# A new priority table and new TensorE costs for the list schedule of an attention and feed-forward kernel

## The chip, the core and the metric

The kernel runs on one core of a Trainium2 chip. The metric is the device time of one execution in microseconds. Three runs of the kernel before gave 746.95, 749.21 and 749.82 us, a median of 749.21. TensorE (PE in the profile) multiplies and writes to PSUM, VectorE (DVE), ScalarE (ACT) and GpSimd (POOL) do the rest, and SyncE (SP) issues most transfers.

## The reference, cut to what matters

For each of 8 batches and 8 heads (576 tokens, width 64, 32 memory slots):

```
a     = softmax(phi) over the tokens          # 576 x 32
k_m   = a^T k ;  v_m = a^T v                  # 32 x 64 each: the memory
attn  = softmax(q k_m^T / 8) over the slots   # 576 x 32
x     = attn v_m                              # 4608 x 512 over all heads and batches
out   = relu(x w_in)^2 w_out                  # w_in 512 x 2048, w_out 2048 x 512
```

The two weight matrices arrive as 64-bit floats and are decoded on the chip.

## The kernel before, in words

The program is written as a list of 3692 operations with their reads and writes. An operation has for each engine that may run it a cost in nanoseconds (`ways`), and a function that issues its instructions. Nothing is issued when an operation is declared: `Plan.order` schedules the whole list in Python while the kernel is built, and the instructions are then issued in the order found. So the costs never reach the chip. They decide three things: the order of the instructions on each engine, the engine where an operation has a choice, and how many filler matmuls go in.

`forward` is a greedy list scheduler. It takes the engine that can start something first, and on it, among the operations whose inputs and buffers are ready, the one with the lowest rank. Where it finds TensorE idle, the gap is noted, and `emit` puts a filler matmul of 512 columns (`fill`, tile `idle`) in for every 260 or 400 ns of it.

In the kernel before, the ranks come from several places. A first rank is worked out backwards from due times; six rounds of `forward` and `backward` improve it; then the table `PLACES` (1600 numbers, start times of some earlier schedule) replaces the ranks of the first 1600 operations, and six more rounds follow. The best schedule of all is issued.

The work itself: for each batch `memory` (twice, four heads each) makes k_m and v_m: a maximum by DVE, two transposes by TensorE (L570, L573), an exponential, the sums (L594; L591 for batches 0 and 1), 20 matmuls on tiles of 32 columns (L582), and two transposes (L616 or L625, and L629). Batches 0 and 1 then run `attention_turned` (transposes of q L682 and L691, scores L710 and L699, transposes of the result L725 and L733), batches 2 to 7 `scores` (L793, tiles of 64 columns, four operations a batch) and `attention`. `vw` multiplies v_m into a slice of w_in (L754, tiles of 64 rows and 32 columns). `mm1` then is six matmuls of 256 or 320 columns into one of two PSUM banks `h` (L864), followed by relu and square on ACT or DVE; `mm2` multiplies by w_out into four banks `acc` (L899, L900, L902), and `mm2_left` does the last 64 tokens of two batches (L925). `decode` turns a piece of the weights from 64 to 32 bits with several DVE and ACT operations (L500 to L516). For batches 2 to 7 the PSUM results of `memory`, `scores` and one half of `vw` share a single bank, tag `pa.0`.

Of the kernel before, what the change touches and what calls it, by code (L numbers as in the profile page):

```python
# [20 lines left out]
P = 128  # L21
# [6 lines left out]
FIRST = 1100  # L28
# [9 lines left out]
AHEAD = 2000  # L38
BEGIN = {"PE": 1000.0, "DVE": 1100.0, "ACT": 800.0, "POOL": 2100.0, "SP": 800.0}
# [94 lines left out]


class Op:
    __slots__ = ("ways", "fn", "deps", "users", "late", "cap", "left", "start", "gap", "lead", "port", "size", "seq", "slack", "code")


class Plan:  # L140
# [930 lines left out]
```

## Time and profile before

| | us |
|---|---|
| median of three runs | 749.21 |
| the profiled execution, its own time | 749.23 |
| its span, first to last instruction | 747.3 |
| TensorE matmul busy | 733.1 (98%) |
| VectorE busy | 513.4 (69%) |
| ScalarE busy | 311.1 (42%) |

The span is 1.9 us shorter than the execution's time. Matmuls are pipelined: one lasts 0.40 us in the trace and the next starts 0.23 us after it, so busy time says that TensorE had something in flight, and the spacing of starts says how fast it went.

### The profile page before, as it was taken

To read this page: it belongs to the slowest core of one execution; us is meant where nothing else is said; L and a number is where in the kernel's file an instruction comes from. 1 tells how busy PE (TensorE), PEld (TensorE's weight loads), DVE (VectorE), ACT (ScalarE), POOL (GpSimd) and SP (SyncE) were. 2 spreads that over 40 slices of the span, in tenths; PEclk is the share of its full clock that TensorE was granted. 3 is DMA by queue.
4 is the path that set the end of the run, shared out by engine and by line. 5 is a ranking of instruction groups with operands and counts; after the bars stand their busy time and mean duration, and the time that the engine had idled before them with its cause. 6 is when DMAs were issued, how large, how long until landed. Compare 5 with 4: busy or idle time off the path is not lost.

```text
span 747.3 us, 13089 instructions
## 1 busy us (share of the span) xinstructions
PE 733.1 (98%) x5004; PEld 586.9 (79%) x5009; DVE 513.4 (69%) x1200; ACT 311.1 (42%) x723; POOL 56.6 (8%) x132
## 2 busy tenths in 40 slices
PE   7899999999999999999999999999999999999997
PEld 4568888888878887788868888687877888788886
DVE  4889998944677677846767666955677576775551
ACT  3467997845422323523423323423242342443320
POOL 2000000010010000400014000120003200040000
PEclk9999999999999999999999999999999999999999
DMA  9994545260640036400363015410344102220002
GB/s 235 239 255 115 167 145 144 89 172 16 171 148 17 1 81 152 104 1 1 106 154 90 1 52 135 105 46 1 80 115 120 36 1 65 61 58 0 1 1 70
DMA packets 59997, 66.38 MB, mean 89 GB/s; under 512 B 18400, under 2 KB 48096, under 8 KB 59936
## 3 DMA queue, kind: packets, MB, share of 16 engines
q1 hardware_dynamic: 55904, 56.77, 30.0%
q0 software_dynamic: 3552, 8.13, 4.2%
q8 instruction: 39, 0.64, 0.4%
q10 hardware_dynamic: 480, 0.66, 0.4%
q14 instruction: 22, 0.18, 0.1%
HBM read 56.10 MB, written 9.44 MB: 88 GB/s over the span
## 4 chain that ended last, share of the span: by engine, by line
PE 92%; DMA 1%; ACT 0%; DVE 0%; issue 0%; ACTq 0%
PE h L864 28%; PE acc L899 16%; PE acc L902 16%; PE acc L900 16%; PE accl L925 6%; PE vwpv L754 4%; PE psc L793 2%; PE pkv L582 2%; DMA raw<-in_moe_w_out_dram 1%; PE psc L710 1%; PE pq L682 0%; PE vwpa L754 0%; PE pvt L625 0%; PE pvt L629 0%; PE pkv L594 0%; PE pmx L570 0%
## 5 line engine op out<-in xcount | busy, mean ns | idle before, releaser
L864 PE MATMUL h<-ath,vw 128*128 128x320 f32 (+1 forms) x1024 | 208.9, 298 | 0.9 <-ACT r L868 0.9
L899 PE MATMUL acc<-wo,gh 128*128 128x512 f32 x512 | 205.4, 401 | 0.0
L900 PE MATMUL acc<-wo,gh 128*128 128x512 f32 x512 | 201.0, 393 | 0.0
L864 PEld LDWEIGHTS h<-ath,vw 128*128 128x128 f32 x1024 | 168.6, 189 | 29.2 <-issue 7.2
L902 PE MATMUL acc<-wo,glo 128*128 128x512 f32 x512 | 159.9, 399 | 0.0
L870 ACT ACTIVATE gh<-r 128x512 fp32r<-128x512 f32 x128 | 81.0, 633 | 151.3 <-DVE r L869 116.2
L899 PEld LDWEIGHTS acc<-wo,gh 128*128 128x128 f32 x512 | 96.3, 188 | 28.2 <-issue 8.1
L902 PEld LDWEIGHTS acc<-wo,glo 128*128 128x128 f32 x512 | 91.9, 189 | 24.7 <-issue 7.5
L900 PEld LDWEIGHTS acc<-wo,gh 128*128 128x128 f32 x512 | 96.5, 188 | 17.2
L864 PE MATMUL h<-atl,vw 128*128 128x320 f32 (+1 forms) x512 | 109.5, 295 | 0.0
L869 DVE TENSOR_SCALAR r<-h 128x256 f32<-128x256 f32 (+1 forms) x104 | 47.4, 456 | 75.2 <-PE h L864 74.4
L868 ACT ACTIVATE r<-h 128x256 f32<-128x256 f32 (+1 forms) x152 | 61.2, 410 | 89.2 <-PE h L864 80.3
L874 DVE TENSOR_TENSOR glo<-r,gh 128x512 fp32r<-128x512 f32 x128 | 88.0, 687 | 13.7 <-ACT r L872 9.7
L864 PEld LDWEIGHTS h<-atl,vw 128*128 128x128 f32 x512 | 82.3, 189 | 0.0
L873 DVE TENSOR_TENSOR r<-r 128x576 f32<-128x576 f32 x69 | 52.2, 757 | 28.9 <-ACT gl L871 26.4
L961 POOL DMA_DIRECT2D out_dram<-o x84 | 41.4, 501 | 195.8 <-ACT o L428 187.4
L925 PE MATMUL accl<-wo,gl 128*128 128x512 f32 x192 | 48.0, 396 | 0.0
L925 PEld LDWEIGHTS accl<-wo,gl 128*128 128x128 f32 x192 | 35.5, 188 | 11.5 <-issue 4.0
L872 ACT ACTIVATE r<-r 128x576 f32<-128x576 f32 x59 | 40.5, 686 | 1.2
L754 PE MATMUL vwpv<-wi,VT 64*32 64x512 f32 (+1 forms) x264 | 34.9, 588 | 0.7 <-DVE wi L510 0.7
L754 PE MATMUL vwpa<-wi,VT 64*32 64x512 f32 (+1 forms) x264 | 34.9, 588 | 0.0
L871 ACT ACTIVATE gl<-r 128x64 fp32r<-128x64 f32 x128 | 31.5, 246 | 4.8 <-DVE r L869 4.5
(133 smaller groups left out, 700.9 us busy)
## 6 DMA issues: line engine op xcount, KB each, us to landing
raw<-in_moe_w_out_dram SPq DMA_DIRECT2D x16, 512.0 KB, 3.6
KV<-in_v_dram SPq DMA_DIRECT2D x16, 512.0 KB, 5.6
KV<-in_k_dram SPq DMA_DIRECT2D x16, 512.0 KB, 4.3
raw<-in_moe_w_in_dram SPq DMA_DIRECT2D x32, 256.0 KB, 4.3
q<-in_q_dram SPq DMA_DIRECT2D x24, 304.0 KB, 4.4
q<-in_q_dram SPq DMA_DIRECT2D x24, 240.0 KB, 3.9
out_dram<-o POOLq DMA_DIRECT2D x80, 64.0 KB, 2.0
phi<-in_phi_dram SPq DMA_DIRECT2D x16, 256.0 KB, 5.7
```

Source lines behind the costliest of these rows:

```text
L754: nc.tensor.matmul(ps_[hh]()[32 * s:32 * s + 32, 0:n], V()[pr, s, :], W()[pr, s, c0:c0 + n], start=True, stop=True, tile_position=(64 * hh ...
L864: nc.tensor.matmul(p()[:, 0:n], V()[:, l, hh, c0:c0 + P], x()[:, hh, cs], start=(i == 0), stop=(i == 5))
L868: op({"ACT": act(n), **({} if b < 2 else {"DVE": tt(n)})}, lambda e, cs=cs, n=n, p=p: nc.scalar.activation(r()[:, cs], p()[:, 0:n], AF.Rel ...
L869: else nc.vector.tensor_scalar(r()[:, cs], p()[:, 0:n], 0.0, None, ALU.max), [p], [(r, h)])
L870: op({"ACT": act(SM)}, lambda e: nc.scalar.activation(gh(), r()[:, 0:SM], AF.Square), [r], [gh])
L873: else nc.vector.tensor_mul(r(), r(), r()), [r], [r], port=BOTH)
L874: vec({"DVE": tt(SM)}, lambda e: nc.vector.tensor_sub(glo(), r()[:, 0:SM], gh().bitcast(F32)), [r, gh], [glo])
L899: nc.tensor.matmul(a(), gh()[:, c], t()[:, 0], start=f0, stop=False)
L900: nc.tensor.matmul(a(), gh()[:, c], t()[:, 1], start=False, stop=False)
L902: nc.tensor.matmul(a(), glo()[:, c], t()[:, 0], start=False, stop=f1)
L925: nc.tensor.matmul(a(), G()[:, l, :], t()[:, w], start=(ff == 0 and n == 0), stop=(ff == NFF - 1 and n == 2))
L961: d(rows, o()[32 * j:32 * (j + n), :])
```

## The change

No operation is added or removed, and no dependency. The costs of TensorE's operations are altered, a field `mode` names the kind of tile that an operation uses (0 the full array, 1 transposes and small full-array products, 2 tiles of 64 rows, 3 tiles of 32 columns, 4 tiles of 64 columns), and `forward` adds time when the kind changes. The rounds of `forward` and `backward` are gone: there is a table of 3692 numbers, a permutation of 0 to 3691, one for each operation, and one pass of `forward` with them as ranks.

```
+SWITCH = (
+    (0, 10, 85, 85, 85),
+    (90, 0, 85, 85, 85),
+    (100, 60, 0, 85, 85),
+    (100, 60, 85, 0, 85),
+    (100, 60, 85, 85, 0),
+)
...
     def order(self):
-        for o in reversed(self.ops):
...
-        rank = {o: PLACES[o.seq] * 10.0 if o.seq < len(PLACES) else best[1][o] for o in self.ops}
-        for _ in range(ROUNDS):
-            found = self.forward(rank)
-            if found[0] < best[0]:
-                best = found
-            rank = self.backward(found)
-        self.last, start, engine, gap = best
+        rank = {o: PLACES[o.seq] for o in self.ops}
+        self.last, start, engine, gap = self.forward(rank)
...
                 words += o.code
+                t += SWITCH[mode][o.mode]
+                mode = o.mode
...
-        op({"PE": 60}, lambda e: nc.tensor.transpose(pm()[:, 0:P], mx()[:, 0:P], ident), [mx], [pm], lead=True)
+        op({"PE": 30}, lambda e: nc.tensor.transpose(pm()[:, 0:P], mx()[:, 0:P], ident), [mx], [pm], lead=True, mode=1)
...
-        op({"PE": 180 if asum else 530}, sums, [asum or A], [pk], lead=True, code=4 if asum else 82)
-        op({"PE": 1190}, mm, [A, KV, pk], [pk], lead=True, code=82)
+        op({"PE": 120 if asum else 480}, sums, [asum or A], [pk], lead=True, code=4 if asum else 82, mode=1 if asum else 3)
+        op({"PE": 1230}, mm, [A, KV, pk], [pk], lead=True, code=82, mode=3)
...
-        op({"PE": 180 + 1.64 * n}, mm, [V] + [(W, (j, h)) for j in js for h in (0, 1)], ps_, lead=True, code=66)
+        op({"PE": 170 + 1.66 * n}, mm, [V] + [(W, (j, h)) for j in js for h in (0, 1)], ps_, lead=True, code=66, mode=2)
...
-            op({"PE": 680 if n < 10 else 790}, mm, [qT, (kb, hh)], [pq], lead=True, code=9)
+            op({"PE": 583 if n < 10 else 690}, mm, [qT, (kb, hh)], [pq], lead=True, code=9, mode=4)
...
-            op({"PE": 713 if n == 256 else 875}, mm, [V] + [(x, (hh, h)) for x in (ah, al) for hh in (0, 1)], [p], code=13)
+            op({"PE": 712 if n == 256 else 876}, mm, [V] + [(x, (hh, h)) for x in (ah, al) for hh in (0, 1)], [p], code=13)
...
-                op({"PE": 235 * (2 - l)}, mm, [glo if l else gh, (t, 0)] + ([] if l else [(t, 1)]), [a], cap=due(g) + 600 * i + 2000 * l, code=4 - 2 * l)
+                op({"PE": 229 * (2 - l)}, mm, [glo if l else gh, (t, 0)] + ([] if l else [(t, 1)]), [a], cap=due(g) + 600 * i + 2000 * l, code=4 - 2 * l)
...
-            op({"PE": 700}, mm, [G, (t, 0), (t, 1)], [a], cap=due(g + 2) + 690 * ff, code=6)
+            op({"PE": 691}, mm, [G, (t, 0), (t, 1)], [a], cap=due(g + 2) + 690 * ff, code=6)
```

The other transposes go from 60 to 30 with `mode=1`; the four operations of L699 get `mode=2`; the rest of `attention_turned` gets `mode=1` at its old costs.

## Rows read from the trace of the kernel before

**Rows 1.** The page: busy time of TensorE, and its granted clock in 40 slices.
```profile
PE 733.1 (98%) x5004; PEld 586.9 (79%) x5009; DVE 513.4 (69%) x1200; ACT 311.1 (42%) x723; POOL 56.6 (8%) x132
...
PEclk9999999999999999999999999999999999999999
```

**Rows 2.** Busy time by stretch: first the stretch, then each engine, clock, DMA share, GB/s.
```profile
0.00:10.00 10.00, 8.80 (x27) 3.10 (x27) 4.61 (x13) 3.70 (x6) 3.14 (x15) 1.00 0.86 233
...
0.00:30.00 30.00, 23.60 (x276) 13.51 (x279) 18.08 (x45) 10.73 (x20) 4.85 (x20) 1.00 1.03 229
30.00:51.00 21.00, 18.38 (x269) 12.22 (x264) 19.36 (x55) 11.48 (x25) 0.71 (x3) 1.00 1.10 264
...
0.00:51.00 51.00, 41.98 (x537) 25.72 (x543) 37.44 (x100) 22.21 (x45) 5.56 (x23) 1.00 1.06 243
51.00:743.00 692.00, 691.09 (x4470) 561.15 (x4468) 475.96 (x1101) 288.31 (x678) 51.05 (x109) 1.00 0.30 78
```

**Rows 3.** Busy time by stretch, filler matmuls (L454) alone.
```profile
0.00:10.00 10.00, 8.50 (x25) 3.06 (x25) 1.00 0.86 233
...
0.00:51.00 51.00, 19.61 (x66) 7.59 (x71) 1.00 1.06 243
51.00:743.00 692.00, 0.00 (x0) 0.00 (x0) 1.00 0.30 78
```

**Rows 4.** What TensorE waited for, 51 to 743 us: total, times, longest.
```profile
PE h L864 <- ACT r L868: 0.9, 2, 0.5
```

**Rows 5.** The end in order of time: start, duration, what came before.
```profile
743.03 0.58 ACT L428 COPY ol<-accl 128x512 f32<-128x512 f32 x1 [15.29 <-PE accl L925]
```

**Rows 6.** TensorE in order of time around one `vw`: start, duration.
```profile
301.90 0.40 PE L899 MATMUL acc<-wo,gh 128*128 128x512 f32 x1
302.13 0.39 PE L900 MATMUL acc<-wo,gh 128*128 128x512 f32 x1
302.45 0.61 PE L754 MATMUL vwpv<-wi,VT 64*32 64x512 f32 x1
...
303.47 0.50 PE L899 MATMUL acc<-wo,gh 128*128 128x512 f32 x1
303.81 0.40 PE L900 MATMUL acc<-wo,gh 128*128 128x512 f32 x1
```

**Rows 7.** Busy time, 51 to 743 us: `vw` L754, `scores` L793, `memory` L582.
```profile
51.00:743.00 692.00, 33.76 (x496) 5.61 (x496) 1.00 0.30 78
...
51.00:743.00 692.00, 16.94 (x96) 4.74 (x96) 1.00 0.30 78
...
51.00:743.00 692.00, 15.59 (x480) 12.37 (x480) 1.00 0.30 78
```

**Rows 8.** TensorE and VectorE in order of time around one `scores`.
```profile
283.04 0.65 PE L793 MATMUL psc<-qT,kb 128*64 128x256 f32 x4
...
284.51 0.41 DVE L797 STREAM_TRANSPOSE S<-psc 128x256 f32<-128x256 f32 x1
```

**Rows 9.** What VectorE waited for, 0 to 51 us.
```profile
DVE work L500 <- DMA raw<-in_moe_w_out_dram: 4.3, 2, 3.4
DVE mx L562 <- DMA phi<-in_phi_dram: 2.4, 1, 2.4
```

**Rows 10.** VectorE, then TensorE, in order of time ahead of the first `mm1`.
```profile
36.31 0.42 DVE L562 TENSOR_TENSOR mx<-phi 128x256 f32<-128x256 f32 x1
...
41.88 0.82 DVE L574 TENSOR_TENSOR phi<-phi,pmx 128x640 f32<-128x640 f32 x1
...
43.10 0.66 DVE L730 TENSOR_TENSOR atl<-pat,ath 128x512 fp32r<-128x512 f32 x1
...
44.18 0.48 PE L864 MATMUL h<-ath,vw 128*128 128x256 f32 x2
```

**Rows 11.** The chain that ended last, batch 1's scores: start, length.
```profile
53.74 2.00 PE psc L710 x16
...
60.24 1.93 PE psc L710 x16
```

More of the change, by code (lines that the diff above doesn't have):

```diff
@@ L136 @@
 class Op:
-    __slots__ = ("ways", "fn", "deps", "users", "late", "cap", "left", "start", "gap", "lead", "port", "size", "seq", "slack", "code")
+    __slots__ = ("ways", "fn", "deps", "users", "late", "cap", "left", "start", "gap", "lead", "port", "size", "seq", "slack", "code", "mode")
 class Plan:
@@ L161, in buf, with op @@
         return b
-    def op(self, ways, fn, r=(), w=(), lead=False, cap=None, port=None, size=0, code=2):
+    def op(self, ways, fn, r=(), w=(), lead=False, cap=None, port=None, size=0, code=2, mode=0):
         o = Op()
-        o.ways, o.fn, o.lead, o.cap, o.port, o.size, o.code = ways, fn, lead, cap, port or {}, size, code
+        o.ways, o.fn, o.lead, o.cap, o.port, o.size, o.code, o.mode = ways, fn, lead, cap, port or {}, size, code, mode
         deps = set()
@@ L199, in order @@
     def order(self):
-        for o in reversed(self.ops):
-            e = min(o.ways, key=o.ways.get)
-            cost = FIRST + o.size / WIRE + LANDS[e] if o.size else o.ways[e] + LAT[e]
-            late = min((u.late for u in o.users), default=1e9)
-            if o.cap is not None:
-                late = min(late, o.cap)
-            o.late = late - cost
-        rank = {o: o.late - (LEAD if o.lead else 0) for o in self.ops}
-        best = None
-        for _ in range(ROUNDS):
-            found = self.forward(rank)
-            if best is None or found[0] < best[0]:
-                best = found
-            rank = self.backward(found)
-        rank = {o: PLACES[o.seq] * 10.0 if o.seq < len(PLACES) else best[1][o] for o in self.ops}
-        for _ in range(ROUNDS):
-            found = self.forward(rank)
-            if found[0] < best[0]:
-                best = found
-            rank = self.backward(found)
-        self.last, start, engine, gap = best
+        rank = {o: PLACES[o.seq] for o in self.ops}
+        self.last, start, engine, gap = self.forward(rank)
         for o in self.ops:
@@ L234, in forward @@
         last = 0.0
-        words, pages = 67, {}
+        words, pages, mode = 67, {}, 0
         def add(o):
@@ L301, in forward @@
         return last, start, engine, gap
-    def backward(self, found):
-        last, start, engine, _ = found
-        free = {e: 0.0 for e in BEGIN}
-        wire = 0.0
-        waiting = {e: [] for e in free}
-        ready = {e: [] for e in free}
-        left = {o: len(o.users) for o in self.ops}
-        when = {o: 0.0 for o in self.ops}
-        rank = {}
-        def settle(e):
-            w, q = waiting[e], ready[e]
-            while w and w[0][0] <= free[e]:
-                o = heapq.heappop(w)[2]
-                heapq.heappush(q, (-start[o], -o.seq, o))
-        for o in self.ops:
-            if not left[o]:
-                heapq.heappush(waiting[engine[o]], (0.0, -o.seq, o))
-        while len(rank) < len(self.ops):
-            best = None
-            for e in free:
-                settle(e)
-                if ready[e]:
-                    t = free[e]
-                elif waiting[e]:
-                    t = waiting[e][0][0]
-                else:
-                    continue
-                if best is None or t < best[0]:
-                    best = t, e
-            t, e = best
-            free[e] = t
-            settle(e)
-            o = heapq.heappop(ready[e])[2]
-            t, d = free[e], o.ways[e]
-            free[e] = end = t + d
-            if o.size:
-                wire = max(wire, t + LANDS[e]) + o.size / WIRE
-                end = wire + FIRST
-                if e == "SP":
-                    free[e] = max(free[e], wire - LANDS[e] - AHEAD)
-            rank[o] = last - end
-            for p in o.deps:
-                left[p] -= 1
-                lat = 0 if p.size or e == engine[p] == "PE" else LAT[engine[p]]
-                when[p] = max(when[p], end + lat + (o.slack if e == "PE" and engine[p] != "PE" else 0))
-                if not left[p]:
-                    heapq.heappush(waiting[engine[p]], (when[p], -p.seq, p))
-        return rank
 def tt(n):
@@ L569, in memory @@
         pm = pt(bank, f"pmx{u}")
-        op({"PE": 60}, lambda e: nc.tensor.transpose(pm()[:, 0:P], mx()[:, 0:P], ident), [mx], [pm], lead=True)
+        op({"PE": 30}, lambda e: nc.tensor.transpose(pm()[:, 0:P], mx()[:, 0:P], ident), [mx], [pm], lead=True, mode=1)
         mc = st([P, 1], F32, "mc", f"mc{u}")
         vec({"DVE": 200}, lambda e: nc.vector.tensor_reduce(mc(), pm()[:, 0:P], AX.X, ALU.max), [pm], [mc], port=None, lead=True)
-        op({"PE": 60}, lambda e: nc.tensor.transpose(pm()[:, P:2 * P], mc().broadcast_to([P, P]), ident), [mc, pm], [pm], lead=True)
+        op({"PE": 30}, lambda e: nc.tensor.transpose(pm()[:, P:2 * P], mc().broadcast_to([P, P]), ident), [mc, pm], [pm], lead=True, mode=1)
         vec({"DVE": tt(640)}, lambda e: nc.vector.tensor_sub(
@@ L615, in memory @@
             op({"POOL": 250}, lambda e: nc.gpsimd.memset(kb(), 0.0), [], [kb], lead=True)
-            op({"PE": 60}, lambda e: nc.tensor.transpose(pv()[:, P:2 * P], two(0), ident), [kx], [(pv, 1)], lead=True)
+            op({"PE": 30}, lambda e: nc.tensor.transpose(pv()[:, P:2 * P], two(0), ident), [kx], [(pv, 1)], lead=True, mode=1)
             for x in (0, 1):
@@ L624, in memory @@
             kb = kTs[b]
-            op({"PE": 60}, lambda e: nc.tensor.transpose(pv()[:, P:2 * P], two(0), ident), [(kx, 0)], [(pv, 1)], lead=True)
+            op({"PE": 30}, lambda e: nc.tensor.transpose(pv()[:, P:2 * P], two(0), ident), [(kx, 0)], [(pv, 1)], lead=True, mode=1)
             vec({"DVE": tt(P)}, lambda e: nc.vector.tensor_mul(
@@ L628, in memory @@
                 [(pv, 1)], [(kb, hh)], port=None, lead=True)
-        op({"PE": 60}, lambda e: nc.tensor.transpose(pv()[:, 0:P], two(1), ident), [kx if b < 2 else (kx, 1)], [(pv, 0)], lead=True)
+        op({"PE": 30}, lambda e: nc.tensor.transpose(pv()[:, 0:P], two(1), ident), [kx if b < 2 else (kx, 1)], [(pv, 0)], lead=True, mode=1)
         pr = slice(64 * hh, 64 * hh + 64)
@@ L682, in mm @@
                         nc.tensor.transpose(pq()[:, y * P:(y + 1) * P], Q()[:, 2 * x + y // 2, 2 * (y % 2):2 * (y % 2) + 2, :].rearrange("p c d -> p (c d)"), ident)
-                op({"PE": 440}, mm, [Q], [pq], lead=True, code=9)
+                op({"PE": 440}, mm, [Q], [pq], lead=True, code=9, mode=1)
                 op({"ACT": act(SM), "DVE": tt(SM)}, lambda e, x=x, pq=pq, qT=qT: copy(
@@ L691, in mm @@
                     nc.tensor.transpose(pq()[0:64, y * LEFT:(y + 1) * LEFT], QL()[:, y, :], ident[0:LEFT, 0:LEFT])
-            op({"PE": 440}, mm, [QL], [pq], lead=True, code=9)
+            op({"PE": 440}, mm, [QL], [pq], lead=True, code=9, mode=1)
             op({"ACT": act(256), "DVE": tt(256)}, lambda e, pq=pq, ql=ql: copy(e, ql(), pq()[0:64, 0:256].rearrange("p (h t) -> p h t", h=4)), [pq], [kl], lead=True)
@@ L700, in mm @@
                                      start=True, stop=True, tile_position=(0, 64 * hh))
-            op({"PE": 500}, mm, [kl, kb], [pq], lead=True, code=17)
+            op({"PE": 500}, mm, [kl, kb], [pq], lead=True, code=17, mode=2)
             op({"ACT": act(P), "DVE": tt(P)}, lambda e, pq=pq, hh=hh: copy(e, Sl()[64 * hh:64 * hh + 64], pq()[64 * hh:64 * hh + 64, 256:384]), [pq], [(rest, 2 + hh)], lead=True)
@@ L710, in mm @@
                         nc.tensor.matmul(s4[:, 2 * y:2 * y + 2, h, :], qT()[:, h, y, :], kb()[:, h].rearrange("p c m -> p (c m)"), start=True, stop=True)
-            op({"PE": 1900}, mm, [qT, kb], [psc], lead=True, code=33)
+            op({"PE": 1900}, mm, [qT, kb], [psc], lead=True, code=33, mode=1)
             Sm = st([P, NMAIN * P], F32, "S", f"S{u}", 2)
@@ L725, in mm @@
                     nc.tensor.transpose(pat()[:, c * P:(c + 1) * P], Sm()[:, c * P:(c + 1) * P], ident)
-            op({"PE": 440}, mm, [Sm], [pat], lead=True, code=9)
+            op({"PE": 440}, mm, [Sm], [pat], lead=True, code=9, mode=1)
             ks = [[(t, (hh, h)) for h in (0, 1)] for t in (ah, al)]
@@ L732, in attention_turned @@
         pat = bank(f"patl{b}")
-        op({"PE": 60}, lambda e: nc.tensor.transpose(pat()[:, 0:P], Sl(), ident), [rest], [pat], lead=True)
+        op({"PE": 30}, lambda e: nc.tensor.transpose(pat()[:, 0:P], Sl(), ident), [rest], [pat], lead=True, mode=1)
         src = lambda: pat()[:, 0:P].rearrange("p (h t) -> p h t", h=2)
```

219 rows, old and new, of the table PLACES are left out of this document.

## The prediction, made before the result was known

> **What bounds the kernel now.** I began with the page. TensorE has something in flight for 98% of the span, and its clock is at the top level, 2.4 GHz, in all 40 slices [rows 1]. So I asked where TensorE could be saved time at all, and cut the span by the windows view into three stretches [rows 2]. From 51 to 743 us TensorE is busy for 691.09 of 692 us. The waits of that stretch add up to 0.9 us, two waits of the first feed-forward product for a relu, the longest 0.5 us [rows 4]. Before 51 us it is busy for 41.98 us, but 19.61 of these are filler matmuls, which compute nothing [rows 3]. Idle and filler together are 51 - 41.98 + 19.61 = 28.6 us. The last copy starts at 743.03 [rows 5]; it, the stores behind it and the end of the program take the last 4.3 us. The reader is to see a start with 28.6 us that TensorE doesn't use, a long middle without a hole, and a short tail.
>
> The change issues the same instructions in another order. In the middle an order can save only what it costs to go from one kind of work to the next. At the start it can save waiting.
>
> **The middle: changes of tile kind.** Full-array matmuls of 512 columns follow each other at 302.13 - 301.90 = 0.23 us. The first matmul of a `vw` starts 0.32 us after the last full one, 0.09 more. After it, the second full matmul starts 303.81 - 303.47 = 0.34 us after the first, 0.11 more [rows 6]. So one excursion to small tiles costs about 0.20 us beside its own work. From 51 to 743 us there are 496/16 = 31 of `vw`, 96/4 = 24 of `scores` and 480/40 = 12 of `memory` [rows 7], 67 in all, 67 x 0.20 = 13.4 us.
>
> The new planner knows of these costs, so it could set two excursions side by side and save one return, 0.11 us, each time. In pairs that is 33 x 0.11 = 3.6 us; in one kind of group or another perhaps 4.5. That is one bound; the other is nothing. I take a value near nothing, 0.2 us, for a reason that is in the code and a row. In batches 2 to 7 all of them write the one bank `pa.0`. Two can't stand side by side unless VectorE empties the bank in between, and the row shows what that takes: a `scores` that starts at 283.04 and lasts 0.65 is emptied from 284.51 to 284.92 [rows 8]. A second excursion right behind would wait 284.92 - 283.69 = 1.2 us to save 0.11. The transposes of `memory` write the same bank.
>
> The altered costs (235 to 229, 60 to 30 and the like) cost nothing by themselves, since they are numbers in the planner.
>
> **The tail.** The copy and stores follow the last matmul whatever the order. Nothing.
>
> **The start.** Here the order can pay, with 28.6 us. The first 10 us can't be had: 8.50 us of them are fillers [rows 3] while the first `phi` comes in. That leaves some 19 us between 10 and 51. What fills them must be ready, and readiness comes from VectorE and the transfers. VectorE is busy for 18.08 - 4.61 = 13.5 of the 20 us from 10 to 30, and for 19.36 of the 21 us from 30 to 51 [rows 2]. Its idle time there, 6.5 + 1.6 = 8.1 us, bounds what a better order can gain: if VectorE never waited, all behind it would come 8.1 us sooner. Most of its waits before 51 us are for transfers, 4.3 + 2.4 = 6.7 us [rows 9], with the DMA engines at a share of 1.03 to 1.10 [rows 2]. So the bytes don't come faster, only in another order, and not all of the 8.1 can be had.
>
> Two more rows give a size. Between 36.31 and 42.6 us VectorE runs ten operations of batch 1's `memory`, the first and the last of which are shown; from start to next start they take 3.3 us, and the last conversion of batch 0's attention waits behind them until 43.10, with the first `mm1` at 44.18 [rows 10]. Put behind, they would let the first `mm1` start some 3 us sooner. And batch 1's two blocks of scores, 2.00 and 1.93 us of TensorE time, run at 53.74 and 60.24, when TensorE is already full [rows 11]; in the holes before 51 they would cost nothing. The table speaks for one and against the other: it gives the second of these blocks the number 152, ahead of many operations that start before 40 us now, but gives the ten operations of batch 1 the numbers 0 to 223 and that conversion 266, so it doesn't ask for them to be put behind. The numbers are priorities, not an order: in 13,460 of the 81,551 pairs in which one operation must wait for another, the waiting one has the lower number. I can't read the order from them.
>
> So the start is bounded by a gain of 8.1 us below. Above, an order that feeds TensorE worse could lose as much as the hole of one late transfer, 3.4 us [rows 9]. I take half of the gain's bound, 4.1 us, which also lies near the 3.3 and the 3.9 us of the two cases.
>
> **The sum**, against the profiled execution's own 749.23 us (span 747.3, 1.9 outside it; 0.02 above the median): start -4.1, middle -0.2, new waits 0, tail 0: 744.9 us.
>
> **Rivals.**
>
> *The start stays as long as it is.* Transfers are the bound before 51 us; VectorE's waits are for them, and a new order only chooses which one is waited for. For it: the DMA share of 1.06 over the 51 us. Against it: VectorE has 1.6 us of waiting left from 30 to 51 us, and there the order of its own work decides. Then the time is 749.2 less 0.2 to 1 us: 748.6, between 747 and 751.
>
> *Slower: the first product waits for relu.* `mm1` has two PSUM banks `h`; the third half in a row waits until ACT or VectorE has emptied the first. This happens twice now, at about 0.45 us [rows 4]. An order with so many inversions may run the halves of two steps closely together, in 128 steps. Nine such waits use up the gain of 4.1 us; at twenty the time is 749.2 - 4.1 + 9 = 754. Against it: `forward` takes only ready operations, and `mm2` matmuls of 0.23 us are there to fill.
>
> *The excursions do get grouped.* If the bank allows more than I think (`vw` also uses another, and batches 0 and 1 have more banks), the middle gives up to 3.6 us beside the start's 4.1: 741.3. By the rows a change costs 0.09 and 0.11. The Trainium skill, in "TensorEngine Tiling (Array Packing)", Key Properties, says that a change of tiling mode drains TensorE. A matmul lasts 0.40 us and the next starts after 0.23, so a full drain would cost an estimated 0.17 each way, 22.8 us for 67 excursions instead of 13.4, and pairs would save 33 x 0.17 = 5.6 us; the time would be 739.3. The trace shows about half of that drain.
>
> **How the numbers follow.** The likeliest case, a shorter start, gets 0.55 and holds 740 to 747; the start that stays gets 0.23; the waits 0.15; the grouping 0.07. The predicted time is 744.9. The range 739 to 752 leaves out the waits and a little at either end, about 0.18. A measurement of this kernel tells about 0.5% from no change, 3.7 us, so the bounds are 745.5 and 753. Faster: 0.40 of the likeliest case and the grouping's 0.07, 0.47. No change: 0.15 of the likeliest case and 0.22 of the second, 0.37. Slower: the waits and 0.01 of the second, 0.16.
>
> **What would show it.** If I am right, the fillers, all of them before 51 us now [rows 3], end some 4 us earlier, or idle and filler before the full stretch fall from 28.6 to about 24.5 us; the waits from there on stay near 1 us; an excursion still costs 0.20 us and there are still about 67 that stand alone; the last matmul ends near 739 us in the span, with 4.3 us behind it. The step on the start is wrong if idle and filler stay at 28; the step on the middle is wrong if `vw` and `scores` stand side by side, or if waits for relu add up to more than 4 us. The whole is wrong if TensorE is no longer full from 51 us on: then VectorE, busy for 475.96 of the 692 us [rows 2], hands it work too late.

## The result, and the profile after

The changed kernel takes 752.98 us (median of 13 runs, 749.03 to 757.91), the kernel before, run beside it, 749.21 us (13 runs, 745.77 to 750.39). The ratio is 1.0053, 95% interval 1.0028 to 1.0078. The prediction was 744.9 us, with 752 as its upper bound: wrong in sign and, by 1 us, outside its range.

The runs of the changed kernel fall into two groups, and the mean granted clock of TensorE in each run tells them apart. Over the three series of it that were made, six runs had a clock of 0.998 or more; their mean is 749.8 us. Seventeen had 0.995 or less; their mean is 754.3 us, 4.5 us more. The kernel before was at 0.994 or more in all of the 75 runs that stood beside these studies, and at 0.998 or more in 47. There the clock goes with less: the 14 runs at 0.995 or less have a mean of 749.2 us, the 47 of 747.8, so a low mean clock alone isn't 4.5 us. The profile after, shown first, is of a run of the first group: 749.81 us, span 748.1. A profile of the second group follows with the first experiment.

The page, answering to [rows 1]:

```profile
PE 732.9 (98%) x5001; PEld 585.9 (78%) x5006; DVE 505.0 (68%) x1185; ACT 321.9 (43%) x738; POOL 56.7 (8%) x132
...
PEclk9999999999999999999999999999999999999999
```

Busy time by stretch, columns as in [rows 2], then the fillers (now L466) alone, as in [rows 3]:

```profile
0.00:10.00 10.00, 7.53 (x33) 3.52 (x34) 4.78 (x14) 3.95 (x7) 2.91 (x15) 1.00 0.85 230
0.00:30.00 30.00, 22.69 (x279) 13.56 (x283) 17.55 (x46) 11.11 (x22) 4.62 (x20) 1.00 1.03 230
...
30.00:51.00 21.00, 18.78 (x265) 12.59 (x266) 19.38 (x54) 11.60 (x27) 0.72 (x3) 1.00 1.12 257
...
0.00:51.00 51.00, 41.47 (x541) 26.15 (x547) 36.92 (x99) 22.72 (x47) 5.33 (x23) 1.00 1.06 241
51.00:743.00 692.00, 690.56 (x4459) 559.40 (x4459) 468.11 (x1087) 298.58 (x691) 51.37 (x109) 1.00 0.30 78
```

```profile
0.00:51.00 51.00, 17.57 (x63) 6.79 (x68) 1.00 1.06 241
```

Idle and filler together before 51 us are 51 - 41.47 + 17.57 = 27.1 us, where they were 28.6: 1.5 won, not 4.1. And these 1.5 us are no more than the kernel before varies by itself. The first 51 us of its second profile (x2 below), all engines and then the fillers alone:

```profile
0.00:51.00 51.00, 43.75 (x551) 27.79 (x556) 38.60 (x102) 24.16 (x50) 5.56 (x23) 1.00 1.06 251
0.00:51.00 51.00, 19.60 (x66) 7.64 (x71) 1.00 1.06 251
```

That is 51 - 43.75 + 19.60 = 26.85 us. VectorE, whose waiting was to be cut, is idle for 20 - (17.55 - 4.78) + 21 - 19.38 = 8.9 us between 10 and 51, where it was 8.1. What VectorE waited for up to 51 us, answering to [rows 9], says which transfer is late now:

```profile
DVE mx L574 <- DMA phi<-in_phi_dram: 4.7, 2, 4.6
DVE work L512 <- DMA raw<-in_moe_w_out_dram: 4.4, 2, 3.7
```

The wait for `phi` grew from 2.4 to 4.7 us (2.3 in the second profile of the kernel before, 4.0 in that of the changed one); that for the output weights stayed at its size (4.3, now 4.4). TensorE in order of time at the first `mm1` (L876 here), which was at 44.18 before [rows 10]:

```profile
41.85 1.30 PE L594 MATMUL pkv<-KV,phi 128*32 128x128 f32 x40
42.94 0.58 PE L603 MATMUL pkv<-ones,phi 128*32 128x1 f32 x38
44.70 0.22 PE L603 MATMUL pkv<-ones,phi 128*32 128x1 f32 x2 [1.18 <-issue]
...
44.94 0.48 PE L876 MATMUL h<-ath,vw 128*128 128x256 f32 x2
```

The first `mm1` starts 0.76 us later than before. Ahead of it is something the kernel before didn't show in its profile: TensorE stands for 1.18 us after 38 of 40 equal matmuls, between two that need nothing from any other engine. "Issue" is the view's word for a wait behind which it sees no releaser. Without the stand the first `mm1` would be 0.4 us sooner, not 3. The second profile of the kernel before has the same stand, shorter:

```profile
43.10 0.23 PE L591 MATMUL pkv<-ones,phi 128*32 128x1 f32 x4 [0.64 <-issue]
```

Batch 1's two blocks of scores, answering to [rows 11]:

```profile
55.26 2.00 PE L722 MATMUL psc<-kb,qT 128*128 128x64 f32 x16
61.38 1.97 PE L722 MATMUL psc<-kb,qT 128*128 128x64 f32 x16
```

Neither came forward into the holes before 51 us; both start 1.1 to 1.5 us later than before.

The long middle: waits from 51 to 743 us, as in [rows 4]; one excursion to `vw`, as in [rows 6]; the counts of `vw`, `scores` and `memory`, as in [rows 7]; and the last copy, as in [rows 5].

```profile
PE pql L703 <- ACT qT L440: 0.7, 1, 0.7
PE psc L805 <- DVE qT L800: 0.3, 1, 0.3
PE acc L914 <- DVE glo L886: 0.3, 1, 0.3
PE h L876 <- ACT r L880: 0.2, 1, 0.2
```

```profile
303.46 0.40 PE L911 MATMUL acc<-wo,gh 128*128 128x512 f32 x1
303.69 0.40 PE L912 MATMUL acc<-wo,gh 128*128 128x512 f32 x1
304.02 0.61 PE L766 MATMUL vwpv<-wi,VT 64*32 64x512 f32 x1
...
305.04 0.50 PE L914 MATMUL acc<-wo,glo 128*128 128x512 f32 x1
305.37 0.40 PE L911 MATMUL acc<-wo,gh 128*128 128x512 f32 x1
```

```profile
51.00:743.00 692.00, 33.87 (x496) 1.00 0.30 78
51.00:743.00 692.00, 16.93 (x96) 1.00 0.30 78
51.00:743.00 692.00, 15.59 (x480) 1.00 0.30 78
```

```profile
743.92 0.59 ACT L440 COPY ol<-accl 128x512 f32<-128x512 f32 x1 [12.52 <-PE accl L937]
```

An excursion costs 304.02 - 303.69 - 0.23 = 0.10 us on the way in and 305.37 - 305.04 - 0.23 = 0.10 on the way out, as before, and there are 67 of them, as before, no two side by side in the order of the trace. The waits add up to 1.5 us instead of 0.9. The last copy starts 0.89 us later than in the profile of before.

### The profile page after: what moved, and what is told of

It reads as the page before. It is cut to its first block, busy times and chain, and to the rows that moved or that the text cites. A ratio compares the mean times of both kernels' runs of the same rounds, so it can differ in the third digit from the quotient of the medians.

```text
span 748.1 us, 13062 instructions
## 1 busy us (share of the span) xinstructions
PE 732.9 (98%) x5001; PEld 585.9 (78%) x5006; DVE 505.0 (68%) x1185; ACT 321.9 (43%) x738; POOL 56.7 (8%) x132
## 4 chain that ended last, share of the span: by engine, by line
PE 87%; DVE 3%; DMA 3%; ACT 1%; issue 1%; SPq 0%; DVEq 0%; ACTq 0%
PE h L876 26%; PE acc L914 16%; PE acc L911 16%; PE acc L912 15%; PE accl L937 6%; PE vwpv L766 4%; PE pkv L594 2%; PE psc L805 2%; DMA q<-in_q_dram 1%; DMA raw<-in_moe_w_out_dram 1%; DVE work L515 0%; DVE qT L800 0%; PE vwpa L766 0%; DVE work L512 0%; DVE wi L522 0%
## 5 line engine op out<-in xcount | busy, mean ns | idle before, releaser
L876 PE MATMUL h<-ath,vw 128*128 128x256 f32 (+1 forms) x1024 | 212.8, 299 | 0.2 <-ACT r L880 0.2
L876 PEld LDWEIGHTS h<-ath,vw 128*128 128x128 f32 x1024 | 169.0, 189 | 27.5 <-issue 4.0
L914 PE MATMUL acc<-wo,glo 128*128 128x512 f32 x512 | 185.7, 400 | 0.3 <-DVE glo L886 0.3
L914 PEld LDWEIGHTS acc<-wo,glo 128*128 128x128 f32 x512 | 94.6, 188 | 28.1 <-issue 6.3
L876 PE MATMUL h<-atl,vw 128*128 128x320 f32 (+1 forms) x512 | 109.6, 295 | 0.0
L881 DVE TENSOR_SCALAR r<-h 128x320 f32<-128x320 f32 (+1 forms) x104 | 47.9, 461 | 57.9 <-PE h L876 56.0
L876 PEld LDWEIGHTS h<-atl,vw 128*128 128x128 f32 x512 | 82.2, 189 | 0.0
L885 DVE TENSOR_TENSOR r<-r 128x576 f32<-128x576 f32 x55 | 41.5, 756 | 40.7 <-ACT gh L882 35.2
L884 ACT ACTIVATE r<-r 128x576 f32<-128x576 f32 x73 | 50.0, 684 | 1.6
L887 DVE TENSOR_TENSOR gl<-r,gl 128x64 fp32r<-128x64 f32 x128 | 28.1, 220 | 11.2 <-ACT r L884 10.2
```

The source lines that it names most:

```text
L876: nc.tensor.matmul(p()[:, 0:n], V()[:, l, hh, c0:c0 + P], x()[:, hh, cs], start=(i == 0), stop=(i == 5))
L881: else nc.vector.tensor_scalar(r()[:, cs], p()[:, 0:n], 0.0, None, ALU.max), [p], [(r, h)])
L884: op({"ACT": act(S), **({} if b < 2 else {"DVE": tt(S)})}, lambda e: nc.scalar.activation(r(), r(), AF.Square) if e == "ACT" else nc.vecto ...
L914: nc.tensor.matmul(a(), glo()[:, c], t()[:, 0], start=False, stop=f1)
```

## The experiments

Two questions were open: what the 4.5 us between the two groups are, and whether the new order costs anything where the clock stays up. The main theory: TensorE's instructions come from memory in pieces; in the new order one piece comes late, TensorE stands about 43 us in, and in most runs the stand is long enough that its clock falls. Rivals: the new order loses the time in the rest of the program; the stand is harmless and the clock falls for another reason. The letters of the theories hold within one expectation each.

**The two kernels once more** (no edit).

> The changed kernel once more, to see its single executions with the granted clock of each. Theory A (clock): the order alone moves the time by less than 1 us, and the slower median comes from executions in which TensorE's clock falls for some 10 us. Then executions at a mean clock of 1.000 take 749 to 750 us, those at 0.99 take 752 to 758, and a profile of such a one shows the low clock in one stretch. Theory B (waits): the new order has waits in the full stretch that vary between executions. Then the time varies at a clock of 1.000 too, or the clock is low because TensorE stood still.

> The kernel before, timed against itself, for the clock of its single executions. Theory A: nearly all at 1.000, times 746 to 750.5 us, ratio 1.000. Theory B says nothing of its clock. If it shows as many executions at 0.99 as the changed kernel, theory A falls.

The changed kernel took 754.91 us, ratio 1.0099 (1.0084 to 1.0113), the kernel before 748.03, ratio 0.9994 (0.9983 to 1.0006). The changed kernel's profile was of the second group. TensorE in order of time in it, and then its busy time and clock by stretch:

```profile
43.31 0.58 PE L603 MATMUL pkv<-ones,phi 128*32 128x1 f32 x38
46.17 0.27 PE L603 MATMUL pkv<-ones,phi 128*32 128x1 f32 x2 [2.27 <-issue]
...
46.49 0.78 PE L876 MATMUL h<-ath,vw 128*128 128x256 f32 x2
```

```profile
44.00:46.00 2.00, 0.00 (x0) 0.81 1.02 214
46.00:48.00 2.00, 1.83 (x9) 0.50 1.16 205
48.00:50.00 2.00, 2.00 (x41) 0.50 1.09 285
50.00:52.00 2.00, 2.00 (x16) 0.50 0.96 293
52.00:54.00 2.00, 2.00 (x17) 0.98 0.22 60
```

The same two matmuls stand for 2.27 us, and TensorE's clock is at 0.50, that is 1.2 GHz, for 6.8 us. It falls at 45.2, while TensorE still stands, and rises at 52.1. A third series of the changed kernel repeats it:

> The changed kernel as it is, on the chip of the three runs above. Theory A: 752 to 755 us with a clock of 0.988 to 0.995 in most executions; any that keeps 0.998 or more takes 749 to 750.5 us. Theory C: the same times, at any clock.

It took 753.83 us, ratio 1.0061 (1.0038 to 1.0084); in its profile the stand is 3.19 us and the clock is at 0.50 from 47.8 us, again within the stand, for 6.8 us. So of three profiles of this program the one with 1.18 us keeps its clock and the two with 2.27 and 3.19 lose it.

**What the stand waits for.** The transfers of the profile have a queue of instructions with 39 or 40 pieces of 16,384 bytes; against about 5,000 matmuls and as many weight loads that is one for every 128 matmuls. In both orders the stand, where there is one, comes ahead of the 466th recorded matmul (the 471st in the third profile of the changed kernel), among the last of those forty; that a piece begins there is inferred from this. This is that piece in the view of transfers, first of the kernel before from 39.8 to 40.2 us, then of the changed kernel from 41.9 to 42.4 (it isn't there from 39.0 to 39.8 and from 39.0 to 41.9):

```profile
q8 instruction: 1, 0.02, 20.3%
```

```profile
q1 hardware_dynamic: 130, 0.13, 114.2%
q8 instruction: 1, 0.02, 17.3%
```

It comes 2 us later, TensorE has used up what it had by 43.5 us, and starts again 2.7 us after the piece began to be fetched; in the five other profiles with this stand it is 2.6 to 2.8 us. The Trainium skill, "Runtime: NRT & Kernel Launch", Instruction fetch mechanics, says that instructions are refilled in blocks of 16 KiB and that crossing a block is mostly hidden. The size agrees; here, with the data queue at a share of 1.14, it isn't hidden: TensorE stands for 1.18 us.

Which part of the order brings it about? Two hybrids of the tables: the old order for the operations of the first 56 us and the new one for the rest, and the reverse; the changed costs with the old table; and the new table in which only the transfers that SP issues keep their old order.

```
...
-PLACES = (10, 11, 1, 16, 21, 15, 47, ...    # the changed kernel
+PLACES = (2, 1, 3, 8, 4, 15, 17, 20, ...    # old start, new rest
+PLACES = (5, 1, 2, 8, 15, 14, 17, 19, ...   # new start, old rest
+PLACES = (10, 11, 1, 16, 13, 15, 47, ...    # new, loads in the old order
...
```

> The operations that the kernel before starts in its planner's first 56 us get ranks in that order; the rest the order of the changed kernel. Theory A, with the fall of the clock brought about by the new order of the start: 746 to 750.5 us and a clock of 1.000 in nearly all executions. Theory B: as slow as the changed kernel, 753 us.

> The reverse: the operations that the changed kernel starts in its planner's first 56 us in its order, the rest in the order of the kernel before. Theory A: a median near 753 us with clocks of 0.99 in most executions. Theory B: as fast as the kernel before, 749 us at a clock of 1.000.

> The new costs and the extra time for changes of tile kind, with the table of 1600 numbers and the rounds of the kernel before. Theory A: the costs do nothing by themselves; what decides is whether TensorE stands at the end of a piece near 43 us: 748 to 750 us if not, 752 to 756 with a clock near 0.993 if so. A third view, that the new costs are what makes the order worse, expects 753 us at a clock of 1.000.

> The changed kernel with the numbers of SyncE's loads handed out anew in the order in which the kernel before issues them. Theory A with the loads as the reason why the piece comes late (in the changed kernel its fetch starts 3 to 4 us after TensorE has entered the piece before, in the kernel before 0.4 to 2.6): the stand gets shorter than 0.7 us, the clock stays at 0.997 or more, and the median is 748 to 751 us. If the order of the loads is not the reason: 753 to 756 us, clock 0.993.

Old start, new rest: 751.58, ratio 1.0047 (1.0033 to 1.0061), between what the two theories expected; a stand of 1.58 us, no fall of the clock between 40 and 100 us. New start, old rest: 756.62, ratio 1.0115 (1.0094 to 1.0137), a stand of 1.99 us and 6.8 us at half clock from 43.7. So the new start suffices for the fall, and the hybrid with the new rest, without a fall, still costs 3.0 us by the medians (751.58 against 748.55). Its stand of 1.58 us is part of that, so not all of it is the rest. Costs alone: 749.36, ratio 1.0018 (1.0008 to 1.0028), no fall after 40 us: the edited costs do little without the new table.

With the loads in the old order the piece is fetched at 39.3 us and the stand at 43 us is gone, as expected. That the order of SP's loads is what delays the piece isn't shown by it: in the hybrid with the old start SP issues its loads up to 44 us in the very same order, and there the piece is fetched at 42.2 and TensorE stands for 1.58 us. What delays the piece stays open. And the time was 755.82, ratio 1.0108 (1.009 to 1.0126), because the same kernel stands elsewhere. Its stands from 70 to 90 us, and its clock:

```profile
76.32 0.30 PE L745 MATMUL patl<-ident,rest 128*128 128x128 f32 x1 [1.11 <-DVE rest L673]
77.63 0.61 PE L766 MATMUL vwpv<-wi,VT 64*32 64x512 f32 x1 [1.01 <-DVE atl L749]
...
80.53 0.90 PE L876 MATMUL h<-ath,vw 128*128 128x320 f32 x2 [1.53 <-ACT vw L440]
```

```profile
78.00:80.00 2.00, 0.99 (x16) 0.58 1.02 301
80.00:82.00 2.00, 1.47 (x5) 0.50 0.68 215
...
84.00:86.00 2.00, 2.00 (x21) 0.71 0.13 26
```

Two shorter stands close together, of 1.11 and 1.01 us and neither of them for instructions, are followed by the same 6.8 us, from 78.3; the third, of 1.53 us, begins at 79.0, when the clock has fallen already. In this profile the clock is at 0.50 also from 57.8 us, for 3.4 us, and in the 4 us ahead of that no stand is longer than 0.34 us. So a late piece is one way to a fall, not the only one, and a long stand isn't needed for each of them.

**Shifting the pieces.** 55 small fillers in the place of five large ones at the start let every later piece begin 50 matmuls earlier in the program, in either kernel (the lines that do it):

```
...
+                fill(n - 5)
+                for _ in range(55):
+                    nc.tensor.matmul(idle[0:32, 0:8], zero.broadcast_to([P, 32]), zero.broadcast_to([P, 8]), start=True, stop=True)
...
```

> The changed kernel with 50 more filler matmuls in TensorE's first wait (five of 512 columns left out, 55 of 8 columns put in), so that every later instruction lies 50 matmuls further on in the instruction stream. Theory A: TensorE's instructions come in pieces of 16,384 bytes, each fetched by DMA while the piece before it runs; at the end of one such piece, at about 43 us, TensorE stands for 1.2 to 2.3 us, just as the full stretch should begin, and in most executions the clock falls to 1.2 GHz for 6.8 us because of it. Shifted, the piece ends elsewhere: no such stand, clock 0.997 or more, a median of 748 to 750 us. Theory C: the new order of the start is less dense anywhere, and the clock falls for that; then the shift does nothing, 753 to 756 us at 0.993.

> The same 50 fillers in the kernel before. Theory A: it loses its own shorter stand (0 to 0.6 us) and takes 747 to 749 us; the shifted changed kernel lies within 1 us of it, since the orders are otherwise worth the same. Theory C: as before, 748.5 us, and the shifted changed kernel 5 us slower.

> The changed kernel with shifted instruction pieces once more, for a second profile: three of its six executions had a mean clock of 0.989 to 0.993, and the one profiled had none of that. Theory A (the clock falls after a stand of some 2 us or more): if the mean clock is below 0.995, a stretch at 0.50 of 6.8 us lies between 40 and 100 us, right behind a stand of 1.9 us or more, not of the instruction piece but of the wait for VectorE's kx, which was 1.59 us in the first profile; if the clock is 0.998 or more, no stand there reaches 1.9 us. Rival (the falls come without such a stand): a stretch at 0.50 with no stand over 1.7 us in the 4 us before it.

> The same kernel a third time, with the same expectations: by theory A a stretch at 0.50 behind a stand of 1.9 us or more, or neither of the two; by the rival a stretch at 0.50 without a stand over 1.7 us in the 4 us before it.

The changed kernel took 751.70, ratio 1.005 (1.0033 to 1.0066), the kernel before 748.19, ratio 1.0009 (0.9999 to 1.0019). The pair missed what the main theory expected in two points, a changed kernel at 748 to 750 us and the two kernels within 1 us of each other. The ratio is inside the interval of the first series of the changed kernel (1.0053) and overlaps that of the third (1.0061); only against the second (1.0099) is it clearly less. So taking the stand away gave back little or nothing that is clear of noise. In three profiles of the changed kernel the stand at 43 us is gone, and none has a fall between 40 us and the last matmul. But three of its six timed runs have clocks of 0.989 to 0.993 and take 752.6 to 753.7 us; none of these was profiled, and where they fall isn't known. Nor are the profiled ones faster than 749.4 us: they are of runs of 750.02, 750.47 and 749.43 us, the last two beside a single 745.86 us of the kernel before. The third one's mean clock is 0.994, and my expectation, that such a clock means a fall between 40 and 100 us, missed: the 6.8 us at half clock begin at 8.2 us.

```profile
8.00:10.00 2.00, 1.56 (x8) 0.54 1.14 269
10.00:12.00 2.00, 1.67 (x9) 0.50 1.20 265
```

There TensorE waits for data anyway, and that run is the shortest of the three. A mean clock tells that TensorE slowed down, not that it cost something; for that one must see where.

> The changed kernel with shifted pieces, six fillers ahead of the turn of the small score tile of batch 0 and seven ahead of the first transposed memory of batch 1's second half (where TensorE stood for 1.59 us at 47.86 us with the pieces shifted). Theory A: no fall of the clock between 40 and 55 us, 0.996 or more in nearly all executions, 749 to 751 us: what then is left against the kernel before, 1 to 2.5 us, is the order itself. Theory C: falls in half of the executions, 751 to 753 us.

This one adds to the shifted pieces six fillers ahead of `patl` of batch 0 and seven ahead of the first of the two transposes of `kx` in one block of batch 1 (the 1.59 us stand at 47.9 us in the first shifted profile). It took 754.11, ratio 1.0082 (1.0062 to 1.0101), where the theory expected 749 to 751. Up to 60 us its profile has one stand left after 42 us, of 0.74, and the clock stays up from 40 us on. Two of its runs keep a clock of 0.998 and still take 753.9 and 754.0 us. Where it loses the time isn't settled; in the profiled run it isn't a fall of the clock after 40 us.

**A stand made in the kernel before.** In batch 0, GpSimd copies the small score tile several times, and TensorE turns that copy ahead of its own turn. This makes a stand of chosen length at the same place, with the old order. The filled variants issue fillers first, which TensorE works through meanwhile.

```
+        def turn(e):
+            if b == 0:
+                held = sb.tile([P, P], F32, tag="held", name="held", bufs=1)
+                nc.gpsimd.tensor_copy(held, Sl())
+                for _ in range(3):              # 7 in the long variant
+                    nc.gpsimd.tensor_copy(held, held)
+                fill(11)                        # filled variants only; 13 in the long one
+                nc.tensor.transpose(pat()[:, P:2 * P], held, ident)
+            nc.tensor.transpose(pat()[:, 0:P], Sl(), ident)
```

> The kernel before, with one thing added: GpSimd copies the small score tile of batch 0 four times when it is ready at about 44 us, and TensorE turns that copy before it goes on, so TensorE stands for some 2.4 us there. Theory A (a stand of about 2 us or more at this place brings the clock down to 1.2 GHz for 6.8 us, and that is what costs): 751 to 754 us, clock 0.993 or less in most executions. Theory C (the new order is less dense in general; one stand does nothing): 748 to 750.5 us, clock 0.997 or more.

> The same delay, but eleven fillers of 512 columns run on TensorE while it waits. Theory A: the delay alone, 1 to 2.4 us at most: 748.5 to 750.5 us, at a clock of 0.997 or more. If the delay itself and not the clock made the run above slow, this is as slow.

The short stand came out at 1.67 us, less than meant: 750.40, ratio 1.0029 (1.0013 to 1.0044), no fall. Filled: 750.62, ratio 1.003 (1.0017 to 1.0044). With no fall there is nothing for fillers to save, and the pair decides nothing about the clock.

> The kernel before, with a longer chain of GpSimd copies ahead of the turn of batch 0's small score tile, so that TensorE stands some 3 us from about 44 us (the shorter chain gave 1.67 us). Theory A (a stand of 2 us and more at this place brings TensorE down to the lower clock, and that costs beside the stand itself): a stretch at 0.50 begins within 3 us of the stand's end, the mean clock of most executions is 0.995 or less, and the time is 752.5 to 755 us against 748.5 for the kernel before. Theory C (the stand does nothing to the clock; the new order's cost has another cause): no such stretch, clock 0.995 and more, and only the delay of the copies is paid: 750 to 752 us.

> The same chain of copies, with 13 matmuls of 512 columns issued ahead of the turn, 13 x 0.217 = 2.8 us, which TensorE works through while it would stand. Theory A: no stretch at 0.50 after 40 us, mean clock 0.997 or more, and 2 to 4 us less than the same chain unfilled, so 750 to 752 us. Theory C: the same time as the chain unfilled, within 0.7 us.

Unfilled: 753.19, ratio 1.0057 (1.0039 to 1.0075). Filled: 751.11, ratio 1.0038 (1.0023 to 1.0053). The six clocks are 0.992 to 0.998 unfilled and 0.998 to 1.000 filled. TensorE in order of time, and busy time and clock by stretch, unfilled:

```profile
44.49 0.58 PE L591 MATMUL pkv<-ones,phi 128*32 128x1 f32 x40
48.15 0.47 PE L739 MATMUL patl<-ident,held 128*128 128x128 f32 x1 [3.08 <-POOL held L738]
```

```profile
46.00:48.00 2.00, 0.00 (x0) 0.88 1.00 169
48.00:50.00 2.00, 1.85 (x8) 0.50 0.33 94
...
52.00:54.00 2.00, 2.00 (x15) 0.50 0.88 302
```

and filled:

```profile
44.20 2.79 PE L454 MATMUL idle<-zero 128*128 128x512 bf16 x12 [0.16 <-issue]
46.83 0.27 PE L740 MATMUL patl<-ident,held 128*128 128x128 f32 x1
```

```profile
46.00:48.00 2.00, 2.00 (x20) 1.00 0.87 185
```

Same order, same chain of copies, same useful work. In a stand of 3.08 us the clock falls, at 47.5, to half for 6.8 us; work that computes nothing in its place prevents that and gains 2.1 us by the medians. With six runs of each, and the intervals of the two ratios overlapping, the size is rough. The rival by which the stand does nothing to the clock is out, for this place and the old order. At half clock the fall can't cost more than half its length, 3.4 us. The Trainium skill, "TensorE: Matmul & The Clock Gate", Terms, gives the penalty as about the time at the lower clock times the share of the clock that is missing, an estimated 3.4 us here too. It cost less in this pair; 0.6 of the 6.8 us still lie in the stand, which ends at 48.15.

## Why the prediction was wrong

**The start, -4.1 us: the step that failed.** It took half of VectorE's 8.1 us of waiting as a gain. That waiting is 8.9 us now. The text itself had the reason, that most of it is for transfers and that the bytes don't come faster, and named "the start stays as long as it is" as a rival. That rival's mechanism is what the profile shows: the wait for `phi` grew by 2.3 us, and idle and filler together fell by 1.5 us, where 4.1 were predicted and where two profiles of the kernel before (28.63 and 26.85) differ by 1.8. The two cases that gave the size show it too. The first `mm1`, put 3 us sooner, starts at 44.94 instead of 44.18, and without its stand at 43.8; batch 1's scores stayed behind 51 us and start at 55.26 and 61.38 instead of 53.74 and 60.24. That 4.1 lay near the size of both cases was no support: neither came about. One sign that the prediction named misled: the last filler starts at 40.99 instead of 50.03 us, 9 us earlier, without such a gain.

**What no step had.** An order decides which instructions stand at a fetch boundary, and which loads the fetch runs against. The stand of 1.2 to 3.2 us there, and the 6.8 us at 1.2 GHz after the longer ones, were in no term and in no rival. By an estimate they make the 4.5 us between the two groups: the stand is longer by 1.1 us (2.27) or 2.0 us (3.19) than in the first group's profile, and the fall adds about 2.1, as measured in the kernel before, and at most 3.4. So 3.2 to 5.4 us. That a stand can bring the fall about is shown in the kernel before; that it is the whole of the changed kernel's loss isn't, since with the pieces shifted the ratio stayed at 1.005. The upper bound of 752 had no term for either: it went up by the hole of one late transfer.

**The middle, -0.2 us, and the tail, 0.** The mechanism was right: 67 excursions remain, each alone, at 0.10 and 0.10 us against 0.09 and 0.11. The grouping rival is out. The waits for relu, the slower rival, are 0.2 us against 0.9: out too, though the sign was slower. New waits, put at 0, are 1.5 - 0.9 = 0.6 us, mostly one for ACT in batch 1's attention. It is there, with 0.7 us, in six of the nine profiles with the new start, and in none of the nine others.

**The sum without the fall.** From the profile: start -1.5, waits +0.6, so -0.9; measured against the profile of before, 749.81 - 749.23 = +0.6. The missing 1.5 us lie in the spread of single runs of the kernel before (745.77 to 750.39), so this pair alone settles nothing. An estimate from the two traces says where they part: with the useful work that is left priced at each kind of matmul's mean spacing after 60 us, the changed kernel is 0.9 us ahead at 51 us, about level at 55, behind the 0.74 us that TensorE waits for ACT, and 0.9 us late at the last matmul. So what was won at the start was gone 4 us later. The series do say more: the shifted kernel's runs at a clock of 0.998 or more take 750.0 to 750.8 against 747.76 beside them, and the old start with the new rest takes 3.0 us more without a fall, a stand of 1.58 us included. The six runs of the changed kernel at such a clock, 749.8, lie 0.6 to 1.2 above the medians beside them (749.21, 748.60). So some 1 to 3 us belong to the new order itself, beside the fall. The wait for ACT is one part; what the rest is stays open: the counts of operations and the excursions of the long middle are as they were.

## What to carry to other kernels

When a planner's order changes, the order of the loads and the place of each instruction among the fetched pieces change with it; look in the profile for a wait without a releaser inside a run of equal matmuls. A wait that leaves TensorE with nothing to do can cost again afterwards by the clock. Fillers in its place gave back some 2 us in the kernel before; in the changed kernel fillers in two places gave back nothing (754.11 us), so time them. And where an engine's idle time is mostly waiting for bytes on queues that are full already, it is no bound of a gain: price only the part that waits for something else.

## What the runs showed of the hardware that was not expected

After 40 us TensorE's clock fell to 1.2 GHz within single stands of 1.99, 2.27, 3.08 and 3.19 us and after two stands of 1.1 and 1.0 us close together; it did not fall at single ones of 1.18, 1.58, 1.59 and 1.67 us. Each of these falls lasted 6.8 us; others lasted 3.4 us, most among the waits of the first 30 us, one from 57.8 us with no stand over 0.34 us ahead of it. A fetch of 16,384 bytes of instructions at about 43 us takes 1.1 to 1.4 us in the profiles while the data queue is full, and where TensorE had to wait for it, it went on 2.6 to 2.8 us after the fetch began.
